# FNet mixing and a gated convolution FFN on one core: weight narrowing spread over two steps, w_in quarters laid end to end, four table loads on another queue

## The chip, the core and the metric

The kernel runs on one core of a Trainium2 chip. The metric is device time in microseconds (us) of one execution. The kernel before was run three times; a further execution was taken by the hardware profiler, and all readings of the trace below are from that one.

## What is computed

Eight sequences of 3136 rows and 256 features (float32) go through a two-dimensional Fourier transform of which the real part is kept, and then through a gated feed-forward layer with a three-tap convolution along the sequence.

```python
X = np.fft.fft(x, axis=1)          # x: (8, 3136, 256)
X = np.fft.fft(X, axis=2)
x = X.real.astype(np.float32)
h = np.maximum(x @ w_in, 0.0)      # w_in: (256, 1024)
hp = pad(h, 1 row on both sides)
conv_out = sum(conv_w[k] * hp[:, k:k + S, :] for k in range(3))
gate = 1.0 / (1.0 + np.exp(-conv_out))
return (h * gate @ w_out)          # w_out: (1024, 256)
```

The activations are float32. The three weight arrays arrive as float64, as pairs of 32-bit words in memory; the kernel turns them into float32 on the chip with integer instructions. This is the "narrowing" below.

## The kernel before, in words

**The work.** For each of the 8 batches the sequence transform is done with matmuls against cosine and sine tables after VectorE has folded the input by symmetry (`fold_ops`, L142). The result lies in two tiles `pt` and `qt` (`PQ[b]`). The transform along the features is multiplied into `w_in` beforehand: `blocks(i)` (L735) multiplies quarter i of `w_in` by the feature tables `dm`, and the product is `G`; `column(i)` (L746) makes the small companion `ge`. One row of the transform is handled apart, by class `Feature` (L468) for batches 1 to 7.

**The main loop** (L1025) runs over steps, one for each batch b, chunk c of the sequence (4 chunks, three of 768 rows and a last one of 832) and block f of 128 hidden features (8 blocks): 256 steps. It is software pipelined. In cycle t these functions are called in this order:

- `sigmoid(t-4)` (L824) on ScalarE
- `products(t+1)` (L777) on TensorE: the two pairs of matmuls into `pb` and `pa`; then `copies(t+1)` (L784) on ScalarE, from `pb` to `nb`
- the side work filed under "first" and "act"
- `combine(t)` (L792) on VectorE, two instructions, giving `h`; `seed(t+2)` (L764) on ScalarE, which starts `pa` of a later step; `first_tap(t)` (L801) on ScalarE, into `g`
- the side work filed under "dve"
- `last_tap(t-3)` (L810) on VectorE; `gate(t-4)` (L830), half on GpSimd (L836), half on VectorE (L837)
- `row_of(t+1)` and `middle(t)` (L806): GpSimd issues a DMA that adds `h` to `g` in SBUF (the middle tap)
- the side work filed under "pool" and "load"
- `mm2(t-5)` (L846): 12 to 14 output matmuls into `po`, and after every eighth step the copies and stores of the results
- the side work filed under "pe"

Each engine takes its instructions strictly in this order of the program, and so does each DMA queue (SP is SyncE's queue, ACTq ScalarE's). The order is written by hand: `at(cycle, where, fn)` (L936) files side work, and `taken` holds the cycles in which VectorE gets no folding of a later batch.

**Around the start of the loop.** `w_in` is narrowed in four quarters (`w4[0..3]`, in two tiles `win` of two quarters each), `w_out` in four pieces of two blocks. `narrow` (L606) has two parts when it is given spare room for the sign: `power` (an integer instruction on VectorE, L620, then a Relu on ScalarE, L622) and `product` (L634 and L635, then L628, which needs the Relu, then L638, all on VectorE). Quarter 1 is narrowed just ahead of the loop, quarter 2 in cycle 0, quarter 3 in cycle 2, and the pieces of `w_out` in cycles 4, 6, 8 and 10: `power` as "first" and `product` as "dve" of the same cycle (L942 to L948). `blocks(1)`, `blocks(2)` and `blocks(3)` come as "pe" in cycles 0, 1 and 3 (L939).

The two quarters of one `win` tile are interleaved: a quarter is two runs of 256 columns, 512 columns apart, one for each half of the contraction:

```python
win = [pqp.tile([P, NK], F32, name="win", tag=tag)[:, 0:F].rearrange("p (t n) -> p t n", t=2)
w4 = [win[i // 2][:, :, i % 2 * N4:(i % 2 + 1) * N4] for i in range(4)]
```

`Feature.place` (L474) is called in cycle 5 under "load". It makes two columns of signs (GpSimd iota L494, VectorE L496, GpSimd L497), clears four short rows on GpSimd (L505) and starts four table loads from ScalarE's queue (L507). `Feature.gather` (L511, on SP) follows in cycles 6 to 8 for batches 1 to 3, element by element; the tables are used from cycle 11 on, the gathered columns in cycle 14.

Of the kernel before, what the change touches and what calls it, by code (L numbers as in the profile page):

```python
# [9 lines left out]
F32 = mybir.dt.float32  # L10
I32 = mybir.dt.int32
U32 = mybir.dt.uint32
AF = mybir.ActivationFunctionType
ALU = mybir.AluOpType
# [16 lines left out]
NQ = 8  # L31
# [6 lines left out]
def kernel(  # L38
# [10 lines left out]
    nc = tc.nc  # L49
    B, S, D = x.shape  # L50
    F = moe_w_in.shape[1]
    P = 128
# [5 lines left out]
    NK = M + 1  # L58
# [17 lines left out]
    pqp = ctx.enter_context(tc.tile_pool(name="pqp", bufs=2))  # L76
# [391 lines left out]
    class Feature:  # L468
# [5 lines left out]
        def place(self):  # L474
            H, t = self.H, erp.tile([P, NK], F32, name="ft", tag="er")
            at_ = [0]

            def take(*sh):
                n = 1
                for v in sh:  # L480
                    n *= v
                v = t[:, at_[0]:at_[0] + n]
                at_[0] += n
                return v
            self.ta = take(2, H + 1).rearrange("p (s k) -> p s k", s=2)
            self.tm = take(2, 2, H).rearrange("p (s r i) -> p s r i", s=2, r=2)
            self.tw = [take(2, 2, H).rearrange("p (s r i) -> p s r i", s=2, r=2) for _ in range(2)]
            self.y = take(4, RC).rearrange("p (b n) -> p b n", b=4)
            self.z = [take(4, 2, RC).rearrange("p (b n) -> p b n", b=4) for _ in range(2)]

            self.sign = take(2)
            odd = self.sign.bitcast(I32)
            for i in range(2):
                nc.gpsimd.iota(odd[:, i:i + 1], pattern=[[0, 1]], base=i, channel_multiplier=1,  # L494
                               allow_small_or_imprecise_dtypes=True)
            nc.vector.tensor_scalar(out=odd, in0=odd, scalar1=1, scalar2=None, op0=ALU.bitwise_and)  # L496
            nc.gpsimd.tensor_scalar(out=self.sign, in0=odd, scalar1=-2.0, scalar2=1.0, op0=ALU.mult, op1=ALU.add)  # L497

            f = t[:, at_[0] - 16 * RC - 2:at_[0] - 2]
            n = (RC + NQ - 1) // NQ  # L500
            self.l = [f[:, 0:2 * HE].rearrange("p (s i) -> p s i", s=2),
                      f[:, 2 * HE:2 * HE + 2 * H].rearrange("p (s i) -> p s i", s=2)]
            for r, v in enumerate(self.l):
                for s in range(2):
                    nc.gpsimd.memset(v[0:1, s], 1.0 - s)  # L505
                    w = v.shape[2]
                    nc.scalar.dma_start(out=v[1:1 + n * NQ, s], in_=bass.AP(  # L507
                        tensor=dft_seq.tensor, offset=dft_seq.offset + (2 * r + s) * NQ * HE,
                        ap=[[4 * NQ * HE, n], [HE, NQ], [1, w]]))

        def gather(self, b, b0):  # L511
            nc.sync.dma_start(out=self.y[self.K, b - b0].unsqueeze(2), in_=bass.AP(
# [93 lines left out]
    def narrow(dst, raw, room=None):  # L606


        ts = nc.vector.tensor_scalar
        lsl, lsr = ALU.logical_shift_left, ALU.logical_shift_right  # L610
        lo, hi = raw[:, :, :, 0], raw[:, :, :, 1]
        lof, d = lo.bitcast(F32), dst.bitcast(I32)
        sg = hi
        if room is not None:
            c, n = hi.shape[1:]
            sg = room[:, 0:c * n].rearrange("p (c n) -> p c n", c=c)

        def power():

            ts(out=d, in0=hi, scalar1=20, scalar2=0x7FF, op0=lsr, op1=ALU.bitwise_and)  # L620
            if room is not None:
                act(d, d, AF.Relu, scale=2.0 ** 23, bias=low[0:d.shape[0]])  # L622
            else:
                ts(out=d, in0=d, scalar1=-896, scalar2=0, op0=ALU.add, op1=ALU.max)
                ts(out=d, in0=d, scalar1=23, scalar2=None, op0=lsl)

        def sign():
            stt(out=d, in0=hi, scalar=-0x80000000, in1=d, op0=ALU.bitwise_and, op1=ALU.bitwise_or)  # L628

        def product():  # L630

            if room is None:
                sign()
            ts(out=sg, in0=hi, scalar1=0xFFFFF, scalar2=0x100000, op0=ALU.bitwise_and, op1=ALU.bitwise_or)  # L634
            stt(out=lof, in0=lo.bitcast(U32), scalar=2.0 ** -32, in1=sg, op0=ALU.mult, op1=ALU.add)  # L635
            if room is not None:
                sign()
            stt(out=dst, in0=lof, scalar=2.0 ** -20, in1=dst, op0=ALU.mult, op1=ALU.mult)  # L638
        return power, product

    class Weight:

# [18 lines left out]
        def narrow(self, c0, c1):  # L661
# [10 lines left out]
                   allow_small_or_imprecise_dtypes=True)  # L672
    nc.gpsimd.tensor_scalar(out=half, in0=half, scalar1=0.5, scalar2=0.5, op0=ALU.mult, op1=ALU.add)
    H = F // 2
    win = [pqp.tile([P, NK], F32, name="win", tag=tag)[:, 0:F].rearrange("p (t n) -> p t n", t=2)
           for tag in ("pt", "qt")]
    w_cv = Weight(cw24, moe_conv_w.rearrange("k (m p) -> (k m) p", m=NF).unsqueeze(1),
                  lambda sh: gp.tile(sh, I32, name="raw", tag="g"))

    dm = gp.tile([P, 2, 2, P], F32, name="dm", tag="g")  # L680
    N4 = F // 4
    w4 = [win[i // 2][:, :, i % 2 * N4:(i % 2 + 1) * N4] for i in range(4)]
    raws = [None, None]

    def raw_in(i):
        def f(sh):
# [5 lines left out]
    w_in = [Weight(w4[i], moe_w_in[:, i * N4:(i + 1) * N4].rearrange("(t p) n -> p t n", p=P), raw_in(i))  # L692
            for i in range(4)]
# [41 lines left out]
    def blocks(i):  # L735

        w = w4[i]
        for g in range(2):
            p = spare()
            for t in range(2):  # L740
                mm(p[:, 0:N4], dm[:, t, g, :], w[:, t], t == 0, t == 1)
            nc.scalar.copy(out=G[:, g, i * N4:(i + 1) * N4], in_=p[:, 0:N4])
        if i > 1:
            column(i)

    def column(i):  # L746

        w, p = w4[i], spare()
        for m in range(NF // 4):
            for t in range(2):  # L750
                mm(p[:, m:m + 1], w[:, t, m * P:(m + 1) * P], dm[:, t, 1, P - 1:P], t == 0, t == 1)
        nc.scalar.copy(out=ge[:, i * NF // 4:(i + 1) * NF // 4], in_=p[:, 0:NF // 4])
# [31 lines left out]
    def copies(s):  # L784

        ch, n, fs = cut(s)
        p = pb.pop(s)
        nb[s] = nbp.tile([P, 2, HN], F32, name="nb", tag="nb")
        for i, cols in enumerate((ch.fcols, ch.cols)):
            act(nb[s][:, i, cols], p[:, cols], AF.Copy, scale=-1.0 if i else 1.0)  # L790
# [107 lines left out]
    for i in range(4):  # L898
        for j, u in enumerate(odds):
            u.part(i)  # L900
            if i == 3:
                u.copy()
                u.fin()
                if j == 1:
                    row()
                    w_out = Weight(wout, moe_w_out.rearrange("(c p) o -> p c o", p=P),
                                   lambda sh: xp.tile(sh, I32, name="raw", tag="xh"))
# [11 lines left out]
    n = chunks[0].k1  # L919
    p = psd.tile([P, 512], F32, name="pd", tag="pd")  # L920
# [7 lines left out]
    room = left[:, NF // 2:].rearrange("p f i -> p (f i)").bitcast(I32)  # L928
# [5 lines left out]
    taken = set()  # L934

    def at(cycle, where, fn):  # L936
        side.setdefault((cycle, where), []).append(fn)

    for i in (1, 2, 3):  # L939
        at((0, 0, 1, 3)[i], "pe", lambda i=i: blocks(i))  # L940

    def shared(cycle, w, c):  # L942
        for where, fn in zip(("first", "dve"), w.parts(c, c + 2, room)):
            at(cycle, where, fn)

    for cycle, w_, c in ((0, w_in[2], 0), (2, w_in[3], 0), (4, w_out, 0), (6, w_out, 2), (8, w_out, 4), (10, w_out, 6)):
        shared(cycle, w_, c)
        taken.add(cycle)  # L948
    for j, fn in enumerate(load_ops(1, 1, nc.sync)):
        at(NF + 3 + max(j - 2, 0), "load", fn)  # L950

# [9 lines left out]

    feat = Feature()
    at(5, "load", feat.place)
    for c, b0, b1 in ((6, 1, min(4, B)), (21, 4, B)):
        for b in range(b0, b1):
            at(c + b - b0, "load", lambda b=b, b0=b0: feat.gather(b, b0))
# [7 lines left out]
    for b in range(1, B):  # L974
# [4 lines left out]
        n = per * b - (2 if b == 1 else 3) - c0  # L979
# [12 lines left out]
    for b in range(1, B):  # L992
        ops, singles, pres = fold_ops(b)
        c0, n = ends[b - 1], ends[b] - ends[b - 1]
# [4 lines left out]
        else:  # L999
            if b == 2:  # L1000
                c0, n = c0 + 3, n - 3
# [16 lines left out]
    n = len(steps)  # L1018
# [2 lines left out]
    seed(steps[1])  # L1021
    products(steps[0])
    copies(steps[0])
    column(1)
    for t in range(n + LAG):  # L1025
        def run(where):
            for fn in side.get((t, where), []):
                fn()
        if 0 <= t - 4 < n:
            sigmoid(steps[t - 4])  # L1030
        if t + 1 < n:
            products(steps[t + 1])
            copies(steps[t + 1])
        run("first")
        run("act")
        if t >= LAG:
            keep(steps[t - LAG])
        if t < n:
            combine(steps[t])
        if t + 2 < n:  # L1040
            seed(steps[t + 2])
        if t < n:
            first_tap(steps[t])

        run("dve")
        if 0 <= t - 3 < n:
            last_tap(steps[t - 3])
        if 0 <= t - 4 < n:
            gate(steps[t - 4])
        if t + 1 < n:  # L1050
            row_of(steps[t + 1])
        if t < n:
            middle(steps[t])
        run("pool")
        run("load")
        if t >= LAG:
            mm2(steps[t - LAG])
        run("pe")
# [66 lines left out]
```

## Time and profile before

| | |
|---|---|
| median of 3 runs | 1173.87 us (1173.63, 1173.87, 1175.4) |
| the profiled execution | 1175.2 us |
| its span in the trace | 1173.4 us |
| TensorE busy with matmuls | 1139.6 us, 97% of the span |
| VectorE, ScalarE, GpSimd busy | 83%, 80%, 52% |
| TensorE clock granted, mean over the span | 0.998 |
| DMA traffic | 168.15 MB, 143 GB/s in the mean |

In the lines quoted below, PE is TensorE's matmuls, DVE VectorE, ACT ScalarE, POOL GpSimd. A line of the timeline has the start in us, the duration in us, the engine, the line of the kernel, the operation with its tiles and shapes, the number of instructions merged into the line, and in brackets the idle time ahead of it with what ended it. All matmuls are issued from L93; their tiles tell them apart: `po<-wout,g` are the output matmuls of `mm2`, `pb<-qt,G` and `pa<-pt,G` those of `products`, `po<-win,dm` those of `blocks`. A line of the waits has the total in us, the number of waits and the longest of them.

### The profile page before, as it was taken

How to read it: one execution, taken by the hardware profiler on the slowest of the kernel's cores; microseconds unless marked ns; L12 is line 12 of the kernel's file. 1: busy time of each engine (PE TensorE's matmuls, PEld its weight loads, DVE VectorE, ACT ScalarE, POOL GpSimd, SP SyncE). 2: the span in 40 equal slices, each digit the busy share in tenths (PEclk: the TensorE clock that was granted, in tenths of full speed). 3: DMA queues.
4: the chain of work that ended last, by engine and by line, in shares of the span. 5: the costliest groups of instructions: out<-in, count | busy, mean ns of one | idle time of the engine just before them, and what ended most of it. 6: DMA issues, size and time to landing. Idle time of an engine off the chain costs nothing.

```text
span 1173.4 us, 15901 instructions
## 1 busy us (share of the span) xinstructions
PE 1139.6 (97%) x4818; PEld 887.5 (76%) x4818; DVE 970.7 (83%) x1448; ACT 942.9 (80%) x1939; POOL 606.9 (52%) x734
## 2 busy tenths in 40 slices
PE   4889999999999999999999999999999999999998
PEld 2756777778778777777777777777778777777777
DVE  7589979998788789798886888889787778788885
ACT  2578868888788888888887878888887888898885
POOL 5346755666465554756455464654344344444443
PEclk9999999999999999999999999999999999999999
DMA  8777787776677676667676676865665656666654
GB/s 209 192 108 156 165 138 165 160 162 135 141 159 168 136 169 141 147 135 176 144 166 139 122 149 141 177 126 121 135 120 107 126 122 142 130 130 129 126 116 102
DMA packets 106050, 168.15 MB, mean 143 GB/s; under 512 B 31121, under 2 KB 61091, under 8 KB 105965
## 3 DMA queue, kind: packets, MB, share of 16 engines
q0 software_dynamic: 41984, 115.83, 51.7%
q1 hardware_dynamic: 62809, 50.88, 15.8%
q8 instruction: 38, 0.62, 0.2%
q10 hardware_dynamic: 1172, 0.43, 0.2%
q14 instruction: 47, 0.39, 0.1%
HBM read 38.40 MB, written 25.74 MB: 55 GB/s over the span
## 4 chain that ended last, share of the span: by engine, by line
PE 77%; ACT 4%; DVE 3%; issue 1%; DMA 0%; POOL 0%; ACTq 0%; DVEq 0%
PE po L93 49%; PE pb L93 12%; PE pa L93 11%; PE pd L93 6%; ACT nb L790 1%; DVE g L813 1%; ACT os L861 1%; ACT g L828 1%; DMA out_dram<-os 0%; ACT pa L769 0%; DVE g L837 0%; DVE w L228 0%; DVE xh L168 0%; ACT g L804 0%; DVE pt L418 0%
## 5 line engine op out<-in xcount | busy, mean ns | idle before, releaser
L93 PE MATMUL po<-wout,g 128*128 128x256 f32 x3072 | 708.3, 380 | 6.6 <-DVE g L837 5.8
L93 PEld LDWEIGHTS po<-wout,g 128*128 128x128 f32 x3072 | 581.6, 190 | 152.5 <-issue 19.7
L808 POOL DMA_DIRECT2D g<-h x256 | 227.7, 889 | 464.5 <-ACT g L804 270.6
L828 ACT ACTIVATE g<-g,cw 128x385 f32<-128x385 f32 (+2 forms) x512 | 292.3, 625 | 68.1 <-DVE g L813 65.5
L836 POOL TENSOR_TENSOR g<-g,h 128x385 f32<-128x385 f32 (+1 forms) x256 | 301.2, 1177 | 49.5 <-ACT g L828 47.9
L790 ACT ACTIVATE nb<-pb 128x386 f32<-128x386 f32 (+3 forms) x512 | 227.3, 499 | 112.1 <-PE pb L93 111.4
L798 DVE CUSTOM_DVE_ANT_0 h<-pa,nb 128x386 f32<-128x386 f32 (+3 forms) x512 | 264.3, 556 | 29.3 <-POOL h L775 19.8
L813 DVE SCALAR_TENSOR_TENSOR g<-h,cw,g 128x770 f32<-128x770 f32 (+1 forms) x256 | 282.8, 1105 | 0.0
L804 ACT ACTIVATE g<-h,cw 128x770 f32<-128x770 f32 (+1 forms) x256 | 244.4, 955 | 0.0
L93 PE MATMUL pb<-qt,G 127*128 127x387 f32 (+2 forms) x512 | 214.0, 499 | 2.6 <-ACT nb L790 1.1
L93 PE MATMUL pa<-pt,G 128*128 128x387 f32 (+2 forms) x512 | 212.3, 495 | 1.2 <-ACT pa L769 1.2
L837 DVE TENSOR_TENSOR g<-g,h 128x385 f32<-128x385 f32 (+1 forms) x256 | 187.0, 730 | 25.0 <-ACT g L828 24.8
L769 ACT ACTIVATE pa<-eb,ge 128x387 f32<-128x387 f32 (+2 forms) x256 | 155.4, 607 | 1.3 <-DVE h L798 1.0
L93 PEld LDWEIGHTS pa<-pt,G 128*128 128x128 f32 x512 | 96.4, 189 | 76.4 <-issue 17.4
L132 POOL DMA_INDIRECT xh<-in_x_dram,idx x64 | 91.1, 1423 | 18.5 <-issue 12.2
L93 PE MATMUL pd<-tab,w 98*128 98x197 f32 (+2 forms) x448 | 98.0, 318 | 0.8 <-DVE w L228 0.7
L93 PEld LDWEIGHTS pb<-qt,G 127*128 127x128 f32 x512 | 90.8, 190 | 9.7 <-ACT nb L790 2.7
L93 PEld LDWEIGHTS pd<-tab,w 98*128 98x128 f32 (+1 forms) x448 | 81.8, 191 | 10.5 <-DVE w L228 1.0
L861 ACT COPY os<-po 128x256 f32<-128x256 f32 x196 | 57.4, 395 | 6.5 <-PE po L93 6.5
L168 DVE TENSOR_TENSOR xh<-xh 98x1024 f32<-98x1024 f32 (+1 forms) x32 | 47.4, 1482 | 0.1
L157 DVE TENSOR_TENSOR xh<-xh 98x1020 f32<-98x1020 f32 (+1 forms) x32 | 46.9, 1471 | 0.0
L385 DVE TENSOR_TENSOR as<-as,pd 128x196 f32<-128x196 f32 x14 | 5.0, 358 | 38.0 <-ACT as L381 38.0
(140 smaller groups left out, 447.7 us busy)
## 6 DMA issues: line engine op xcount, KB each, us to landing
g<-h POOLq DMA_DIRECT2D x192, 385.0 KB, 4.1
g<-h POOLq DMA_DIRECT2D x64, 416.0 KB, 4.4
out_dram<-os SPq DMA_DIRECT2D x96, 256.0 KB
xh<-in_x_dram SPq DMA_DIRECT2D x16, 784.0 KB
eb<-ed SPq DMA_DIRECT2D x16, 193.5 KB
raw<-in_moe_w_in_dram SPq DMA_DIRECT2D x4, 512.0 KB
raw<-in_moe_w_out_dram SPq DMA_DIRECT2D x1, 2048.0 KB
eb<-ed SPq DMA_DIRECT2D x8, 209.0 KB
```

The lines of the kernel that those rows point to most:

```text
L93: nc.tensor.matmul(o, l, r, start=start, stop=stop, skip_group_check=True)
L132: nc.gpsimd.indirect_dma_start(out=xh[b, h][0:NP, 7 - m].rearrange("p q d -> p (q d)"), out_offset=None, in_=bass.AP(tensor=x.tensor, offs ...
L769: act(pa[s][:, 0:n], eb[b, c], AF.Copy, scale=ge[:, f:f + 1])
L790: act(nb[s][:, i, cols], p[:, cols], AF.Copy, scale=-1.0 if i else 1.0)
L798: nc.vector._custom_dve(TENSOR_ADD_SAT, out=to, in0=a[:, cols], in1=c[:, i, cols], s0=BIG, s1=0.0)
L804: act(gs[s], hs[s][:, 0:n], AF.Copy, scale=cw[:, 0, s[2]:s[2] + 1])
L808: nc.gpsimd.dma_start(out=gs[s], in_=hs[s][:, 1:1 + n], accum_op=ALU.add)
L813: stt(out=g, in0=h[:, k:k + n], scalar=cw[:, k, f:f + 1], in1=g, op0=ALU.mult, op1=ALU.add)
L828: act(gs[s][:, c], gs[s][:, c], AF.Sigmoid, scale=cw[:, 1, s[2]:s[2] + 1])
L836: gt(g[:, p], g[:, p], h[:, p], op=ALU.mult)
L837: vt(g[:, v], g[:, v], h[:, v], op=ALU.mult)
L861: nc.scalar.copy(out=osb[:, j % 2], in_=pt[:, j % 2])
```

## The change

It has four parts.

1. The quarters of `w_in` lie one behind the other in their tiles, so that each quarter is one run of 512 columns.
2. `narrow` with room gives three parts in place of two: the last two VectorE instructions (L628 and L638) become `value`, and `value` is filed one cycle after `power` and `product`. For quarter 3 and for `w_out`, `power` and `product` move one cycle earlier (to cycles 1, 3, 5, 7, 9), and `value` takes the cycle where all of it stood (2, 4, 6, 8, 10). For quarter 2, `power` moves ahead of the loop; `product` and `value` stay in cycle 0.
3. `blocks(1)` moves from the end of cycle 0 to ahead of the loop, behind `column(1)`, and so ahead of `products` of step 1.
4. In `Feature`, the four table loads are started from SP's queue; the two sign instructions L496 and L497 are called in cycle 8 under "dve" and no longer in `place`.

```diff
-            nc.vector.tensor_scalar(out=odd, in0=odd, scalar1=1, scalar2=None, op0=ALU.bitwise_and)
-            nc.gpsimd.tensor_scalar(out=self.sign, in0=odd, scalar1=-2.0, scalar2=1.0, op0=ALU.mult, op1=ALU.add)
...
-                    nc.scalar.dma_start(out=v[1:1 + n * NQ, s], in_=bass.AP(
+                    nc.sync.dma_start(out=v[1:1 + n * NQ, s], in_=bass.AP(
...
+        def signs(self):
+            odd = self.sign.bitcast(I32)
+            nc.vector.tensor_scalar(out=odd, in0=odd, scalar1=1, scalar2=None, op0=ALU.bitwise_and)
+            nc.gpsimd.tensor_scalar(out=self.sign, in0=odd, scalar1=-2.0, scalar2=1.0, op0=ALU.mult, op1=ALU.add)
...
             stt(out=lof, in0=lo.bitcast(U32), scalar=2.0 ** -32, in1=sg, op0=ALU.mult, op1=ALU.add)
+            if room is None:
+                value()
+
+        def value():
             if room is not None:
                 sign()
             stt(out=dst, in0=lof, scalar=2.0 ** -20, in1=dst, op0=ALU.mult, op1=ALU.mult)
-        return power, product
+        return (power, product) if room is None else (power, product, value)
...
-    win = [pqp.tile([P, NK], F32, name="win", tag=tag)[:, 0:F].rearrange("p (t n) -> p t n", t=2)
+    win = [pqp.tile([P, NK], F32, name="win", tag=tag)[:, 0:F].rearrange("p (i t n) -> p i t n", i=2, t=2)
...
-    w4 = [win[i // 2][:, :, i % 2 * N4:(i % 2 + 1) * N4] for i in range(4)]
+    w4 = [win[i // 2][:, i % 2] for i in range(4)]
...
-    for i in (1, 2, 3):
+    for i in (2, 3):
         at((0, 0, 1, 3)[i], "pe", lambda i=i: blocks(i))
-    def shared(cycle, w, c):
-        for where, fn in zip(("first", "dve"), w.parts(c, c + 2, room)):
-            at(cycle, where, fn)
-    for cycle, w_, c in ((0, w_in[2], 0), (2, w_in[3], 0), (4, w_out, 0), (6, w_out, 2), (8, w_out, 4), (10, w_out, 6)):
-        shared(cycle, w_, c)
-        taken.add(cycle)
+    early, *rest = w_in[2].parts(0, 2, room)
+    for fn in rest:
+        at(0, "dve", fn)
+    for cycle, w_, c in ((1, w_in[3], 0), (3, w_out, 0), (5, w_out, 2), (7, w_out, 4), (9, w_out, 6)):
+        for j, where, fn in zip((0, 0, 1), ("first", "dve", "dve"), w_.parts(c, c + 2, room)):
+            at(cycle + j, where, fn)
+    taken.update((0, 2, 4, 6, 8, 10))
...
     at(5, "load", feat.place)
+    at(8, "dve", feat.signs)
...
     copies(steps[0])
+    early()
     column(1)
+    blocks(1)
```

## The prediction

> **What bounds the kernel now.** First the shares on the page, to see which engine could set the end.
>
> ```profile
> PE 1139.6 (97%) x4818; PEld 887.5 (76%) x4818; DVE 970.7 (83%) x1448; ACT 942.9 (80%) x1939; POOL 606.9 (52%) x734
> ```
>
> TensorE is the bound nearly everywhere, so a gain must come from the few stretches in which it waits, and the change touches only the ramp and the first eleven steps (about 45 to 100 us). Next, the chain near the end shows what a step costs when TensorE is fed, and TensorE's timeline shows how the early steps differ.
>
> ```profile
> 1103.63 2.59 PE po L93 x12
> 1106.22 0.65 PE pb L93 x2
> 1106.88 0.65 PE pa L93 x2
> ```
>
> ```profile
> 70.23 2.86 PE L93 MATMUL po<-wout,g 128*128 128x256 f32 x12 [1.46 <-DVE g L837]
> ...
> 80.41 4.49 PE L93 MATMUL po<-wout,g 128*128 128x256 f32 x12 [1.97 <-DVE g L837]
> ...
> 98.67 2.86 PE L93 MATMUL po<-wout,g 128*128 128x256 f32 x12 [0.63 <-DVE g L837]
> ...
> 112.08 2.75 PE L93 MATMUL po<-wout,g 128*128 128x256 f32 x12
> ```
>
> A fed step takes 2.59 + 0.65 + 0.65 = 3.89 us. The first output matmuls (step 0) start at 70.23, those of step 6 at 98.67: 28.44 us for six steps where 23.3 would do, so 5.1 us are lost. From 98.67 to 112.08, three steps later, 1.7 us more go. Each of the three waits shown names VectorE's half of the gate: in these steps the bound is VectorE. Its waits between 45 and 100 us say why.
>
> ```profile
> DVE win L620 <- PE po L93: 4.9, 2, 3.6
> DVE wout L628 <- ACT wout L622: 2.1, 2, 1.2
> DVE ft L496 <- POOL ft L494: 1.8, 1, 1.8
> DVE win L628 <- ACT win L622: 1.1, 1, 1.1
> ```
>
> That is 9.9 us of standing still on the engine everything waits for. The first row is a write to one quarter of w_in waiting for matmuls that read the other quarter: the quarters interleave, and the order between them is kept as if they overlapped. Rows two and four are the narrowing waiting for its own Relu. Row three is the sign column waiting for GpSimd.
>
> **Part 1, the waits that go.** Laid end to end, the quarters share no range and the first row goes. Of its 4.9 us, 3.6 are the wait of quarter 3, which stops VectorE in cycle 2. The other 1.2, ahead of the loop, gain almost nothing: the Relu stands on ScalarE behind copies that end when it now starts. With value one cycle later, the Relu has a whole cycle, so rows two and four (3.2 us) go. Signs in cycle 8 find their iota done (1.8 us). What does VectorE need without waits?
>
> ```profile
> 80.28 1.02 DVE L798 CUSTOM_DVE_ANT_0 h<-pa,nb 128x385 f32<-128x385 f32 x2
> ...
> 82.70 0.41 DVE L620 TENSOR_SCALAR wout<-raw 128x512 int32<-128x512 int32 x1
> ...
> 93.46 0.41 DVE L620 TENSOR_SCALAR wout<-raw 128x512 int32<-128x512 int32 x1
> ...
> 98.53 1.02 DVE L798 CUSTOM_DVE_ANT_0 h<-pa,nb 128x386 f32<-128x386 f32 x2
> ```
>
> A plain step runs from 80.28 to 82.70, 2.42 us; a step with a whole narrowing and no wait from 93.46 to 98.53, 5.07. Two steps take 7.49, or 3.75 each, and the split spreads this evenly. That is just below TensorE's 3.89. So once the waits are gone, TensorE takes over as the bound. What is late next is ScalarE, in the ramp.
>
> **Part 2, the ramp.** Here the change adds something: blocks(1) now stands ahead of the products of step 1.
>
> ```profile
> 51.06 1.89 PE L93 MATMUL po<-win,dm 128*128 128x256 f32 x8
> 51.37 0.72 ACT L622 ACTIVATE win<-win,low 128x512 int32<-128x512 int32 x1
> 51.98 0.59 ACT L769 ACTIVATE pa<-eb,ge 128x386 f32<-128x386 f32 x1
> 52.13 0.69 DVE L628 SCALAR_TENSOR_TENSOR win<-raw,win 128x512 int32<-128x512 int32 x1 [1.15 <-ACT win L622]
> 52.49 0.94 ACT L804 ACTIVATE g<-h,cw 128x770 f32<-128x770 f32 x1
> 52.85 0.69 DVE L638 SCALAR_TENSOR_TENSOR win<-raw,win 128x512 f32<-128x512 f32 x1
> 53.32 0.64 ACT L742 COPY G<-po 128x256 f32<-128x256 f32 x2
> ```
>
> The 1.89 us push the products of step 1, their copies, the seed and the first tap back; 0.3 us from the earlier narrowing and the 0.7 of the Relu, which leaves its place ahead of the seed, come off. The first tap of step 0 then starts near 53.3 in place of 52.49: 0.8 us lost, the price of this edit. From there I laid the engines out by hand with the spacing of ScalarE's instructions in a stretch where it never waits:
>
> ```profile
> 116.70 1.11 ACT L828 ACTIVATE g<-g,cw 128x385 f32<-128x385 f32 x2
> 117.72 0.85 ACT L790 ACTIVATE nb<-pb 128x386 f32<-128x386 f32 x2
> 118.46 0.57 ACT L769 ACTIVATE pa<-eb,ge 128x387 f32<-128x387 f32 x1
> 118.97 0.93 ACT L804 ACTIVATE g<-h,cw 128x770 f32<-128x770 f32 x1
> 119.80 1.11 ACT L828 ACTIVATE g<-g,cw 128x385 f32<-128x385 f32 x2
> ```
>
> Start to start: sigmoid 1.02, copies 0.74, seed 0.51, first tap 0.83. From the first tap of step 0 to the end of the first tap of step 4, which is followed by sigmoid(1), ScalarE has 5 taps (4.15), 4 pairs of copies (2.96), 4 seeds (2.04), 2 Relus (0.6 each to the next start, 1.2), 2 sets of copies of G with ge (1.6) and one sigmoid (1.02): 13.0 us. Hence sigmoid(1) near 66.3, the seed of step 6 done near 65.6, its products near 66.5, and the output matmuls of step 0 right behind, at **66.5 in place of 70.23: 3.7 us** gained. VectorE's half of gate(0) lands near 66.3 by the same layout, so neither is far ahead. Bounds: 70.23 + 0.8 if ScalarE alone had set the old ramp, 65.6 if nothing of the ramp waited for TensorE. I take 66.5 because ScalarE is laid out back to back.
>
> **Part 3, steps 0 to 6.** From there TensorE should run at 3.89 a step. Of the 5.1 us lost before I keep 1.0: one refill, and one wait in step 10, because in step 9 a fold instruction of batch 1 falls in with power, product and an ordinary step on VectorE. Step 6 then starts near 66.5 + 23.3 + 1.0 = 90.8, **4.1 us** gained. The ends are 0 (all lost again to something else) and 5.1. The stretched 4.49 us at 80.41 belong to it: the granted clock was halved there.
>
> ```profile
> 76.00:80.00 4.00, 2.45 (x9) 1.21 (x7) 3.93 (x6) 2.41 (x6) 1.81 (x3) 1.00 0.20 35
> 80.00:84.00 4.00, 3.59 (x9) 2.91 (x10) 4.00 (x9) 4.00 (x8) 1.43 (x2) 0.57 0.53 99
> ```
>
> The columns are PE, PEld, DVE, ACT, POOL busy, then the granted clock, which is 0.57 in the second stretch after one in which TensorE was busy 2.45 of 4 us. The 12 matmuls took 4.49 in place of 2.86, 1.63 more. Without the wait of 1.97 ahead of it the first stretch is full and this goes too. The Trainium skill, "TensorE: Matmul & The Clock Gate" (Part 1), has the clock drop only after about a whole 3.4 us window of idleness; by that rule this drop should not have come at all, and the trace goes against it. By the rule the changed kernel runs at full clock throughout, as in my sum; by the trace it could be halved wherever TensorE is half idle, which is a rival below.
>
> **Part 4, what I cost at nothing.** Four table loads move to SP's queue, ahead of the gathers.
>
> ```profile
> L507 ACTq DMA_DIRECT2D ft<-dft_seq_dram x4: 761/782/862, 71.2 to 73.7; - x4
> ```
>
> ```profile
> L512 SPq DMA_DIRECT2D ft<-in_x_dram x3: 902/5281/7396, 49.2 to 57.6; - x3
> ```
>
> Four issues of 0.78 us leave ScalarE, 3.1 us. They add nothing to my sum because ScalarE is not the bound by then; if it is, they are a gain of up to 3.1. On SP they go out near 49 us, when SP is already free, and push the three gathers back by 3.1 us; these are read only in cycle 14, and behind them SP has nothing until the load of cycle 11. Without that cover the price is 3.1 us once. L497 now makes GpSimd wait for VectorE in cycle 8, and its half of gate(4) and the tap's DMA queue behind it; VectorE has last_tap and its own half to do meanwhile, which hides it. The layout changes no duration: every quarter keeps 512 columns an instruction. Value one cycle later still ends a cycle ahead of the output matmuls that use it.
>
> **The sum.** 3.7 + 4.1 = 7.8 us, against the profiled execution's own 1175.2: **1167.4**. Later steps are bound by TensorE, so the gain stays. The profiled execution lies 1.3 us above the median of 1173.87; the halved clock may be that difference, or not. If it is, 1167.4 holds as it stands; if the profile simply costs 1.3, it is 1166.1. Best case: the ramp gains 3.7, all 5.1 come back, and the 1.7 of steps 6 to 9 too, 10.5 us, or 1164.7.
>
> **The rivals.**
>
> A: the clock is halved once more, in the thinner ramp. Price 1.63, time 1169.0. For it: the row above. Against: the layout has TensorE busier than before in each stretch from 52 us on.
>
> B: the middle tap's DMA becomes the late one.
>
> ```profile
> DMA to landing us min/median/max: 7.3/7.3/7.3
> ```
>
> That is the tap of step 0, issued while the gathers run. The gathers now end 3.1 us later, so the next two taps also meet them, and VectorE asks for each tap earlier. In the layout the tap of step 1 lands within half a microsecond of its use. If landings grow by the 3.1, the ramp gives 3 us back: 1170.4.
>
> C: the change doesn't do what it says: quarters stay tied to each other by tile and not by range. Then blocks(2) waits for the Relu of quarter 3, about 1.2 us later on TensorE, and ScalarE's chain inherits it: 1168.6.
>
> D: VectorE stays the bound, because its integer instructions meet GpSimd.
>
> ```profile
> L634 DVE TENSOR_SCALAR left<-raw x7: 409/419/1524, 46.2 to 94.7; 128x512 int32<-128x512 int32 x7
> ```
>
> The same instruction takes 0.42 in the median and up to 1.52. The slack of 3.89 - 3.75 is 0.14 a step, so three such meetings (1.1 each) more than now cost 3 us: 1170.4. The Trainium skill, "Advanced Engine Details and Errata" (VectorE Performance Modes, Mode Summary), says that VectorE's second port is shared with GpSimd and that two-port instructions block each other; it speaks against filing these instructions in other cycles, and the spread of this row agrees with it.
>
> E, slower: the halved clock feeds itself. Matmuls of the ramp at half speed delay copies, seeds and gates, TensorE idles, and the next stretch is halved too. Each costs about 1.63, so from the fifth on (7.8 / 1.63) the gain is eaten; at seven the time is 1178.8 with no gain elsewhere than forecast. For it: one such stretch exists. Against: it did not repeat even after the 1.97 wait.
>
> **How the numbers follow.** Forecast 0.61 (1164.5 to 1169), A 0.08, B 0.12, C 0.07, D 0.09, E 0.03. A measurement of this kernel tells about 0.2% from no change, 2.3 us. Faster by more: the forecast, A, C, and most of B and D, 0.92. Within: the dear ends of B and D, 0.05. Slower: E, 0.03. The range 1163.8 to 1170.8 takes in the best case with half a microsecond, and B and D at their price.
>
> **What would show it.** VectorE's waits L620 for TensorE, L628 for the Relu and L496 for the iota are gone; output matmuls start near 66.5 and those of step 6 near 90.8; the granted clock stays 1.00 from 20 us on; L507 stands on SP near 49 to 53. I am wrong if the first start is later than 68, if waits of last_tap for its DMA appear, or if VectorE shows no idle time in steps 2 to 9 while TensorE waits for L837.

## The result and the profile after

The changed kernel takes 1170.03 us in the median of 8 runs (1168.57 to 1171.95), the kernel before 1174.61 in 8 runs beside it (1173.62 to 1176.98). The ratio is 0.9959, with a 95% interval from 0.9947 to 0.9971: 4.6 to 4.8 us faster. The profiled execution took 1169.77 us against 1175.2, 5.4 less. The forecast was 1167.4, a gain of 7.8. The sign and the range held; the sum was 2.4 us too large against the profiled execution, and 3.0 to 3.2 against the medians. The median lies above the band of 1164.5 to 1169 that the forecast itself was given, close to the 1170.4 of rivals B and D.

VectorE's waits between 45 and 100 us in the changed kernel, to be held against the four rows of before (line numbers are higher by 4 to 9: L620 is now L624, L628 is L632, L634 is L638, `last_tap` is L822, the gate's halves are L845 and L846):

```profile
DVE g L822 <- DMA g<-h: 1.7, 1, 1.7
DVE win L632 <- ACT win L626: 0.9, 1, 0.9
DVE h L807 <- POOL h L784: 0.8, 1, 0.8
DVE h L807 <- PE pa L93: 0.7, 2, 0.5
```

9.9 us have become 4.1. The four rows of before are gone from the loop: the waits for the matmuls of the other quarter, for the iota, and the two rows for the Relu. Ahead of the loop 0.9 us stand in place of 1.2, now for a Relu that stands behind other copies. The other rows are new: the last tap of step 0 waits 1.7 us for the accumulating DMA, and `combine` (L807) of the first steps waits 1.5 us, for GpSimd's clear of the edges of `h` and for matmuls. Next, TensorE's output matmuls of steps 0, 2, 5, 6 and 9:

```profile
67.59 2.86 PE L93 MATMUL po<-wout,g 128*128 128x256 f32 x12 [0.81 <-DVE g L846]
...
76.40 2.86 PE L93 MATMUL po<-wout,g 128*128 128x256 f32 x12 [0.76 <-DVE g L846]
...
89.86 2.86 PE L93 MATMUL po<-wout,g 128*128 128x256 f32 x12 [1.50 <-DVE g L846]
93.86 2.75 PE L93 MATMUL po<-wout,g 128*128 128x256 f32 x12
...
107.14 2.75 PE L93 MATMUL po<-wout,g 128*128 128x256 f32 x12
```

The first group starts 2.6 us earlier than before (70.23), that of step 6 4.8 us earlier (98.67), that of step 9 4.9 us earlier (112.08). The gain is made before 94 us and then kept. The last output matmuls on the chain that ends last, before and after:

```profile
1147.75 20.73 PE po L93 x96
```

```profile
1142.33 20.73 PE po L93 x96
```

They start 5.4 us earlier. TensorE, busy 97% of the span before and after, passes what is gained in the ramp on to the end, as was forecast.

Between step 0 and step 6 26.27 us pass, where 28.44 passed before, 24.3 were forecast and 23.3 would be the work alone. All three bracketed waits are for VectorE's half of the gate: VectorE is still the bound of these steps, though from 62.2 us on it no longer stands still in them. What holds it is seen when GpSimd's instructions are shown beside its own. The changed kernel, VectorE and GpSimd, as step 6 begins:

```profile
71.78 0.54 POOL L494 IOTA ft<- 128x1 int32 x2
...
71.94 0.90 POOL L503 MEMSET ft<- 1x393 f32 x4
72.12 2.10 DVE L632 SCALAR_TENSOR_TENSOR wout<-raw,wout 128x512 int32<-128x512 int32 x1
...
72.81 0.86 POOL L845 TENSOR_TENSOR g<-g,h 128x385 f32<-128x385 f32 x1
```

L632, the first instruction of `value`, was L628 in the kernel before and needed 0.69 us there for every piece of `w_out` (the times are in ns):

```profile
L628 DVE SCALAR_TENSOR_TENSOR wout<-raw,wout x4: 684/692/696, 67.4 to 95.8; 128x512 int32<-128x512 int32 x4
```

Here it takes 2.10 and ends 0.5 us after GpSimd has finished its clears and its gate. The same again in steps 8 and 9, first GpSimd, then VectorE:

```profile
82.51 0.88 POOL L513 TENSOR_SCALAR ft<-ft 128x2 f32<-128x2 int32 x1 [1.61 <-DVE ft L512]
83.37 1.17 POOL L845 TENSOR_TENSOR g<-g,h 128x385 f32<-128x385 f32 x1
84.48 0.87 POOL L817 DMA_DIRECT2D g<-h  x1
85.09 1.16 POOL L845 TENSOR_TENSOR g<-g,h 128x385 f32<-128x385 f32 x1
```

```profile
83.73 1.09 DVE L624 TENSOR_SCALAR wout<-raw 128x512 int32<-128x512 int32 x1
84.74 1.01 DVE L807 CUSTOM_DVE_ANT_0 h<-pa,nb 128x386 f32<-128x386 f32 x2
85.68 0.86 DVE L638 TENSOR_SCALAR left<-raw 128x512 int32<-128x512 int32 x1
```

The sign instruction makes GpSimd wait 1.61 us for VectorE; its gate of step 4 comes late, the gate of step 5 right behind it, and both lie over integer instructions that take 0.42 us when nothing is beside them. L807 between them, which reads PSUM and one SBUF tile, is not stretched (1.01 us). The size of it all can be added up from VectorE's timeline: from its half of gate(0) at 66.98 to that of gate(5) at 89.25 VectorE works without a gap, 22.3 us for five steps. 2.5 of these are stretch (1.41 in L632, 0.67 in L624, 0.44 in L638); without them a step would take VectorE 3.95 us, beside TensorE's 3.89.

### The profile page after: what moved, and what is told of

Same layout as the page of the kernel before. It is cut to its first block, busy times and chain, and to the rows that moved or that the text cites. A ratio compares the mean times of both kernels' runs of the same rounds, so it can differ in the third digit from the quotient of the medians.

```text
span 1168.0 us, 15901 instructions
## 1 busy us (share of the span) xinstructions
PE 1136.9 (97%) x4818; PEld 886.9 (76%) x4818; DVE 970.5 (83%) x1448; ACT 942.1 (81%) x1939; POOL 610.3 (52%) x734
## 4 chain that ended last, share of the span: by engine, by line
PE 78%; ACT 4%; DVE 3%; issue 2%; DMA 0%; POOL 0%; ACTq 0%; DVEq 0%
PE po L93 49%; PE pb L93 12%; PE pa L93 12%; PE pd L93 6%; ACT nb L799 1%; ACT os L870 1%; DVE g L822 1%; ACT g L837 1%; ACT pa L778 0%; ACT g L813 0%; DMA out_dram<-os 0%; DVE g L846 0%; DVE h L807 0%; DVE w L228 0%; DVE pt L418 0%
## 5 line engine op out<-in xcount | busy, mean ns | idle before, releaser
L845 POOL TENSOR_TENSOR g<-g,h 128x385 f32<-128x385 f32 (+1 forms) x256 | 303.7, 1187 | 49.9 <-ACT g L837 48.2
L807 DVE CUSTOM_DVE_ANT_0 h<-pa,nb 128x386 f32<-128x386 f32 (+3 forms) x512 | 264.6, 557 | 31.2 <-POOL h L784 20.6
L822 DVE SCALAR_TENSOR_TENSOR g<-h,cw,g 128x770 f32<-128x770 f32 (+1 forms) x256 | 282.8, 1105 | 1.7 <-DMA g<-h 1.7
L846 DVE TENSOR_TENSOR g<-g,h 128x385 f32<-128x385 f32 (+1 forms) x256 | 187.2, 731 | 24.8 <-ACT g L837 24.7
```

The costliest lines, as they stand in the source:

```text
L807: nc.vector._custom_dve(TENSOR_ADD_SAT, out=to, in0=a[:, cols], in1=c[:, i, cols], s0=BIG, s1=0.0)
L822: stt(out=g, in0=h[:, k:k + n], scalar=cw[:, k, f:f + 1], in1=g, op0=ALU.mult, op1=ALU.add)
L845: gt(g[:, p], g[:, p], h[:, p], op=ALU.mult)
L846: vt(g[:, v], g[:, v], h[:, v], op=ALU.mult)
```

## The experiments

The theory after the result: the split of the narrowing carries the gain; 1.2 us were lost because the gathers, pushed back by the table loads, make the first tap's DMA late; 2 us because GpSimd's work now lies over VectorE's two-input and integer instructions. The rivals: the layout carried the gain; or what looks like lost time is only step 9, which is long by itself.

The runs of one kernel spread by 2 to 4 us, and the next two fences show a reason. They are the stretch from 32 to 36 us, ahead of everything the change touches, in the changed kernel and in the kernel with the loads back on ScalarE's queue (columns: PE, PEld, DVE, ACT, POOL busy, granted clock, DMA share, GB/s).

```profile
32.00:36.00 4.00, 4.00 (x25) 4.00 (x24) 0.86 (x3) 0.84 (x3) 0.00 (x0) 1.00 0.54 193
```

```profile
32.00:36.00 4.00, 4.00 (x17) 4.00 (x17) 0.00 (x0) 0.00 (x0) 0.00 (x0) 0.67 0.11 41
```

The clock is halved for part of this stretch in the second execution (0.67 in the mean of the 4 us) and not in the first, though both have the same program up to there; the matmuls of the first `column` (`po<-dm,win`) start at 42.77 in the first and at 44.32 in the second, 1.55 us later. Of the 14 profiled executions, 8 had such a stretch in the first 100 us, one of them two. So the times of a few runs do not separate kernels that differ by 1 us, and the readings below rest also on the traces: the start of the output matmuls of step 0 and of step 6, counted from the matmuls of the first `column`. "Ratio" is to the kernel before. The last column is the fastest execution on record of each kernel, in us; its mean granted clock is 0.999 or 1.000 in every kernel, where one stretch takes 0.0015 off (half of 3.4 us in 1168). The kernel before was run beside each group of the others; its fastest there are 1173.42 to 1173.83. The two fastest of a kernel lie within 0.3 us of each other in all but u_signs and signs_dve.

```text
kernel         ratio, 95% interval       step 0   step 6   halved clock, first 100 us   fastest
before         1                         27.32    55.76    at 80                        1173.42
the change     0.9959 [0.9947, 0.9971]   24.82    51.09    none                         1168.57
u_layout       0.9965 [0.9952, 0.9978]   25.00    51.52    at 31, ahead                 1170.08
u_split        0.9990 [0.9981, 0.9999]   26.88    54.57    at 70                        1172.73
u_queue        0.9943 [0.9931, 0.9955]   23.59    49.69    at 31, ahead                 1168.10
u_signs        0.9958 [0.9945, 0.9971]   25.27    51.97    at 44                        1168.95
u_blocks       0.9960 [0.9947, 0.9973]   23.74    50.27    none                         1169.00
q_behind       0.9956 [0.9943, 0.9969]   23.59    50.11    none                         1168.64
place_early    0.9956 [0.9943, 0.9969]   23.59    49.46    none                         1168.08
signs_dve      0.9962 [0.9950, 0.9974]   24.55    50.65    none                         1168.54
cheap_gather   0.9961 [0.9947, 0.9975]   23.59    50.10    none                         1169.05
split_only     0.9974 [0.9964, 0.9984]   26.61    53.30    at 44                        1170.55
best           0.9953 [0.9939, 0.9967]   25.27    50.68    at 43                        1168.25
best_blocks    0.9949 [0.9935, 0.9962]   25.44    50.85    at 32 and 45                 1167.99
```

"Ahead" means ahead of the counted part.

**Which part carries the gain.** First each part undone, the others kept.

```diff
# u_split
-    early, *rest = w_in[2].parts(0, 2, room)
-    for fn in rest:
-        at(0, "dve", fn)
-    for cycle, w_, c in ((1, w_in[3], 0), (3, w_out, 0), (5, w_out, 2), (7, w_out, 4), (9, w_out, 6)):
-        for j, where, fn in zip((0, 0, 1), ("first", "dve", "dve"), w_.parts(c, c + 2, room)):
-            at(cycle + j, where, fn)
+    for cycle, w_, c in ((0, w_in[2], 0), (2, w_in[3], 0), (4, w_out, 0), (6, w_out, 2), (8, w_out, 4), (10, w_out, 6)):
+        for where, fn in zip(("first", "dve", "dve"), w_.parts(c, c + 2, room)):
+            at(cycle, where, fn)
...
-    early()
```

> The change with the narrowing filed as before (power, product and value in one cycle, quarter 2's power in cycle 0), the other parts kept. Theory: VectorE waits for its own Relu again, about 3 us in all, and narrowing steps are long; 2 to 3 us slower than the change, ratio near 0.998. Rival (the split only moved VectorE's work under GpSimd's, and the stretched 2.10 and 1.30 us instructions ate what it gained): within 1 us of the change, ratio 0.996.

The ratio is 0.9990: of the 0.41% that the change gains, 0.31% go, 3.6 us; between the fastest executions it is 4.2. Its trace has the waits that the split takes away:

```profile
DVE win L632 <- ACT win L626: 5.3, 3, 2.9
DVE wout L632 <- ACT wout L626: 2.2, 3, 1.2
```

Step 6 starts 3.5 us later than in the change, with a halved stretch on the way (4.54 for twelve output matmuls in place of 2.86, 1.7 us). The rival, that the split only moved work under GpSimd's, is out.

```diff
# u_layout
-    win = [... .rearrange("p (i t n) -> p i t n", i=2, t=2)
+    win = [... .rearrange("p (t n) -> p t n", t=2)
-    w4 = [win[i // 2][:, i % 2] for i in range(4)]
+    w4 = [win[i // 2][:, :, i % 2 * N4:(i % 2 + 1) * N4] for i in range(4)]
```

> The change with its first part undone: the quarters of w_in interleave again. Theory (the split and the earlier filing already take quarter 3 off the matmuls of the ramp): now blocks(2) waits for the Relu of quarter 3 and value of quarter 3 for column(2), about 1 us on the ramp; 1.0 us slower than the change, ratio to the kernel before near 0.997. Rival (the layout was the main gain, its 3.6 us wait comes back whole): 3 us or more slower than the change, ratio 0.999.

0.9965, 0.7 us slower in the ratio and 0.4 us in the trace at step 6: the theory's side, though the ratios alone do not separate it from the change. The trace makes the layout look too cheap: last_tap of step 0 does not wait for its DMA here, as it does for 1.7 us in the change. Against q_behind below, where that wait is gone too, this kernel is 1.4 us late both at step 0 and at step 6, and its two fastest executions (1170.08 and 1170.10) are 1.5 us slower than the fastest of the change. The waits are back, the 1.2 us ahead of the loop whole, that of quarter 3 short, because it is now filed a step earlier:

```profile
DVE win L632 <- PE po L93: 1.4, 1, 1.4
DVE win L624 <- PE po L93: 1.2, 1, 1.2
```

Of the wait of 3.6 us that the prediction put down to the interleaving, earlier filing alone thus removes most; 1.4 are left, now ahead of `value`. The split alone, with everything else as before:

```diff
# split_only: the kernel before, and of the change only part 2
```

> The kernel before with the second part of the change alone (narrowing over two steps, one step earlier, quarter 2's power ahead of the loop); quarters interleaved, blocks(1) at the end of step 0, loads on ScalarE, signs in the placing. Theory (this part carries nearly the whole gain, and the others give and take within 1.5 us): 4 to 5 us faster than the kernel before, ratio 0.996, like the whole change. Rival (the parts need each other: with interleaved quarters VectorE or TensorE waits in the ramp and the split gains half): ratio 0.998.

0.9974: 3.1 us of the 4.8, between the two expectations; between the fastest executions 3.3 (1173.83 beside it to 1170.55). Its profiled execution has a halved stretch in the ramp, so its step 0 and step 6 are late by some 1.7 us. The split stands without the other parts, and with the 1.4 to 1.5 us of the layout it makes up nearly the whole gain.

**The table loads on SP.**

```diff
# u_queue
-                    nc.sync.dma_start(out=v[1:1 + n * NQ, s], in_=bass.AP(
+                    nc.scalar.dma_start(out=v[1:1 + n * NQ, s], in_=bass.AP(
```

> The change with the four table loads back on ScalarE's queue. Theory (prediction): nothing is lost, since the sigmoid of step 2 waits for VectorE longer than the issues take; within 0.5 us of the change, ratio 0.996. Rival 1: ScalarE is held 1.6 us in step 5 or 6 and the gate of step 2 comes later; 1 to 1.5 us slower, ratio 0.997. Rival 2: the gathers start 3.6 us earlier on SP, the first tap lands earlier, and the kernel is up to 1 us faster than the change.

0.9943, the fastest ratio of all, though its interval meets that of the change; between the fastest executions it is 0.5 us. In the trace step 6 starts 1.4 us earlier than in the change. The wait of last_tap for its DMA is not there. This is rival 2, and in these traces it speaks against a part of the change. SP's queue in the changed kernel, and VectorE at the tap:

```profile
48.41 3.56 SPq L505 DMA_DIRECT2D ft<-dft_seq_dram  x4
52.01 16.91 SPq L516 DMA_DIRECT2D ft<-in_x_dram  x3
```

```profile
62.23 1.02 DVE L822 SCALAR_TENSOR_TENSOR g<-h,cw,g 128x770 f32<-128x770 f32 x1 [1.73 <-DMA g<-h]
```

The gathers run from 52.0 to 68.9 in place of 49.2 to 62.8. The tap's DMA was issued at 54.3 and VectorE goes on at 62.2, 7.9 us later, where the DMA of the kernel before had landed after 7.3. To test the reason, the loads were put behind the gathers:

```diff
# q_behind: the loads of place as a method of their own
+    at(9, "load", feat.loads)
```

> The change with the four table loads on SP behind the three gathers (filed in step 9) instead of ahead of them. Theory (ahead of the gathers they push these 3.6 us later, the accumulating DMA of the first tap lands late under them, and VectorE stands 1.7 us at last_tap of step 0): that wait is gone and the output matmuls of step 0 start about 1.2 us earlier; 1.2 to 1.6 us faster than the change, ratio to the kernel before 0.9945. Rival (the gain with the loads on ScalarE's queue was the chance of that chip): same as the change, 0.996.

```profile
48.31 13.28 SPq L521 DMA_DIRECT2D ft<-in_x_dram  x3
61.63 6.71 SPq L510 DMA_DIRECT2D ft<-dft_seq_dram  x4
```

The wait is gone, step 0 starts 1.2 us earlier and step 6 1.0 earlier in two executions at full clock. The times (0.9956 against 0.9959) do not show it, and the fastest execution of the change, 1168.57, is as fast as that of q_behind, 1168.64. So the change probably does not wait for this DMA in every execution; that is not shown, since no trace here is of one that doesn't. And with the gathers made cheap in pieces (the kernel then reads 56 neighbouring features of every 56th row, and leaves out the one feature of every row that is needed):

```diff
# cheap_gather
-    ap=[[RC * D, RC], [D, RC], [1, 1]]
+    ap=[[RC * D, RC], [1, RC]]
```

> The change with the gathers reading 56 neighbouring elements a row in place of 56 elements a row's length apart: the same bytes in far fewer pieces; it leaves out that the right feature is gathered. Theory (the element-wise gathers make the accumulating DMAs of the first taps land late): the first tap lands within 5 us in place of 7.9, the wait of 1.7 us at last_tap of step 0 is gone, output matmuls of step 0 start near 66.3; 1 us faster than the change, ratio 0.995. Rival (the late landing is the fill of the DMA engines by other loads): the landing stays above 7 us and so does the wait.

The three gathers now take SP 2.9 us in place of 16.9, the wait is gone, and step 0 starts 1.2 us earlier, as with the loads behind them. The ratio, 0.9961, does not show it, against 0.995 expected. The landing itself is not shown in the traces of these three kernels, only the wait. Its length differs between executions: 1.7 us in the change, 1.4 in signs_dve and 0.5 in place_early, with the same order on SP, and each of these kernels has one trace. So the traces side with the theory that the element-wise gathers behind the loads make that DMA late, but how they do it stays open: in q_behind element-wise gathers run beside the same DMA, from 48.3 to 61.6, and VectorE does not wait.

**blocks(1) ahead of the loop.**

```diff
# u_blocks
-    for i in (2, 3):
+    for i in (1, 2, 3):
...
-    blocks(1)
```

> The change with blocks(1) back at the end of step 0, behind the products of step 1. Theory (blocks(1) ahead costs ScalarE's chain 0.6 us at the first tap, and the ramp hangs on ScalarE and the first tap's DMA): 0.5 us faster than the change in the ramp. Rival (behind the products its copies of G hold up the products of step 2, as the 1.1 us wait of TensorE on G in the kernel before): 0.5 to 1 us slower.

Step 0 starts 1.1 us earlier than in the change, step 6 0.8 earlier; the ratio is the same, and the fastest execution is 0.4 us slower. The trace goes in the theory's direction, by more than its 0.5: GpSimd issues the first tap at 52.50 and not at 54.34, so that it lands in time.

```profile
52.50 1.01 POOL L817 DMA_DIRECT2D g<-h  x1 [5.53 <-ACT G L751]
```

In the traces, the loads behind the gathers or back on ScalarE's queue, cheap gathers, and blocks(1) undone thus all take away one and the same wait, 1.1 to 1.2 us at step 0; they do not add up.

**GpSimd beside VectorE.**

```diff
# place_early
-    at(5, "load", feat.place)
...
     blocks(1)
+    feat.place()
```

> The change with the placing (iota, the four clears, the loads) called ahead of the loop, where GpSimd is idle, so that GpSimd has nothing in step 5 but its gate and tap; the signs stay in step 8, SP's order stays. Theory (GpSimd's work of step 5 lies over VectorE's L632 of step 6, which took 2.10 us in place of 0.69): L632 is short again, the wait of 0.8 us ahead of the third output matmuls goes; 0.5 to 0.8 us faster than the change, ratio 0.9955. Rival (TensorE's wait at step 10 absorbs whatever comes earlier): no difference, 0.996, with that wait longer by what was gained.

VectorE in step 6 of this kernel, then TensorE at steps 1, 2 and 5:

```profile
71.58 0.97 DVE L632 SCALAR_TENSOR_TENSOR wout<-raw,wout 128x512 int32<-128x512 int32 x1
```

```profile
70.79 2.86 PE L93 MATMUL po<-wout,g 128*128 128x256 f32 x12 [0.28 <-DVE g L846]
74.79 2.81 PE L93 MATMUL po<-wout,g 128*128 128x256 f32 x12
...
88.22 2.86 PE L93 MATMUL po<-wout,g 128*128 128x256 f32 x12 [1.52 <-DVE g L846]
```

With GpSimd's clears out of step 5, L632 falls from 2.10 to 0.97 and the wait ahead of the third group goes. Step 6 starts 1.6 us earlier: 1.2 at step 0, by the shorter wait for the tap, and 0.4 after it. The wait of step 5's output matmuls does not grow, so the rival (step 10 absorbs the gain) falls. The ratio does not show the gain; the fastest execution is 0.5 us faster. Not all of the stretch is gone: beside GpSimd's earlier gates the last tap of step 1 takes 1.62 us here in place of 1.00, and L638 of step 5 1.12.

```diff
# signs_dve
-            nc.gpsimd.tensor_scalar(out=self.sign, in0=odd, scalar1=-2.0, scalar2=1.0, ...)
+            nc.vector.tensor_scalar(out=self.sign, in0=odd, scalar1=-2.0, scalar2=1.0, ...)
```

> The change with the second sign instruction on VectorE, so that GpSimd waits for nothing in step 8. Theory (GpSimd's gate of step 4, held behind its sign instruction until 83.4, and the next one meet L624 and L638 of step 9 and stretch them by 1.1 us in all): these two are 0.42 us each again, the wait of 1.50 us ahead of the output matmuls of step 5 falls below 0.7; 0.7 to 1.0 us faster than the change, ratio 0.995. Rival (step 9 is long by its fold instruction alone): that wait stays at 1.5 and the time at 0.996.

```profile
80.72 1.42 DVE L632 SCALAR_TENSOR_TENSOR wout<-raw,wout 128x512 int32<-128x512 int32 x1
...
84.45 0.42 DVE L624 TENSOR_SCALAR wout<-raw 128x512 int32<-128x512 int32 x1
84.79 1.02 DVE L807 CUSTOM_DVE_ANT_0 h<-pa,nb 128x386 f32<-128x386 f32 x2
85.73 0.41 DVE L638 TENSOR_SCALAR left<-raw 128x512 int32<-128x512 int32 x1
```

L624 and L638 are short again and the wait ahead of step 5's output matmuls falls from 1.50 to 0.70, as expected. But GpSimd's gate, no longer held back, now meets L632 of step 8, 1.42 in place of 0.68. The gain is 0.4 us at step 6, of which 0.3 stand already at step 0 (a shorter wait for the tap), and not the 0.7 to 1.0 expected; the time shows nothing. A meeting avoided in one step is met in the next. The 0.70 us ahead of step 5 stay in u_signs, best and best_blocks as well, so this part of step 9 is long by itself, as the rival has it.

```diff
# u_signs
+            self.signs()
...
-    at(8, "dve", feat.signs)
```

> The change with the two sign instructions back in the placing of step 5. Theory (in step 8 the GpSimd one holds up the gates behind it, and they then stretch L624 to 1.09 and L638 to 0.86 us): what VectorE loses in step 5 (1.8 us of waiting) it mostly regains in step 9; within 0.7 us of the change. Rival (prediction's reckoning: 1.8 us of wait come back and nothing else changes): 1.5 to 1.8 us slower, ratio 0.9975.

0.9958, the ratio of the change. The theory's side: the move of the signs by itself brings nothing that the ratio shows. Its trace shows VectorE waiting 0.7 us for the iota, where the kernel before waited 1.8.

**Put together.**

```diff
# best: place ahead of the loop, loads behind the gathers, both sign instructions on VectorE
-    at(5, "load", feat.place)
-    at(8, "dve", feat.signs)
+    at(2, "dve", feat.signs)
+    at(9, "load", feat.loads)
...
     blocks(1)
+    feat.place()
```

> The change with GpSimd's placing work ahead of the loop, the table loads on SP behind the gathers, and both sign instructions on VectorE in step 2. Theory: no wait on the first tap's DMA, no long L632 in step 6; the signs cost nothing in step 2; with GpSimd free in step 8 L632 of step 8 is stretched instead of L624 and L638 of step 9; output matmuls of step 0 near 66.3, of step 6 near 92; 1.5 to 2 us faster than the change, ratio 0.9943. Rival (TensorE's wait at step 10 eats it): ratio 0.9955.

> The kernel called best here, with blocks(1) back at the end of step 0. Theory (blocks(1) ahead costs about 1 us in the ramp only where the first tap's DMA is late, since the chain then runs through that tap): with the loads behind the gathers it makes less than 0.5 us, ratio 0.994 as the kernel without this edit. Rival (it costs ScalarE's chain its 0.6 us in any case): 0.6 to 1 us faster, ratio 0.9937.

0.9953 and 0.9949, medians 1169.27 and 1170.13 us, fastest runs 1168.25 and 1167.99 (the change: 1168.57). Both profiled executions had a halved stretch in or ahead of the ramp. From step 0 to step 6 they need 25.4 us, against 26.27 in the change. In the trace of best the wait for the tap's DMA is gone, L632 takes 0.97 in step 6 and 1.43 in step 8, and L624 and L638 of step 9 take 0.42 and 0.41, as expected (all three stand 5 lines lower in this kernel); but L638 of step 5 takes 1.67 in their place. As times, neither is shown to beat the change, and they are not shown to differ from each other.

## Why the prediction was right, and where its sum was off

**What bounds the kernel** held: VectorE's waits in the first eleven steps, and TensorE carrying the gain to the end (4.8 us at step 6, 5.4 at the end). Two of the three signs that the prediction named for being wrong came all the same: last_tap waits for its DMA, and from step 4 on VectorE has no idle time while TensorE waits for its half of the gate. That the time still fell into the range is owed to the width of the range, which takes in rivals B and D.

**Part 1, the waits that go**, held for all four rows. The attribution was too simple: the 3.6 us wait of quarter 3 was put down to the layout; u_layout shows that filing it a step earlier removes most of it. The conclusion that TensorE takes over as the bound once the waits are gone did not hold (Part 3).

**Part 2, the ramp**, said 66.5 and 3.7 us; 67.59 and 2.6 us came. The first tap came at 53.1 where 53.3 was laid out. The step that failed is that no wait for its DMA stands in the layout: VectorE asked for it 6.2 us after the issue (at 60.5) and went on after 7.9, with sigmoid, copies and gate behind it. Already with the 7.3 us of before it would have waited 1.1. Without that wait (q_behind, cheap_gather) step 0 starts near 66.3 to 66.7, where the layout by hand had it. Rival B was thus right in kind, for one tap and with 1.2 us in place of 3.

**Part 3, steps 0 to 6**, is the largest error: "of the 5.1 us lost before I keep 1.0" was 2.9. The work of VectorE was summed with each instruction's undisturbed duration, so that 3.75 us a step came out, below TensorE's 3.89; with 2.5 us of stretch in five steps it was 4.45. Rival D had the right mechanism and named one kind of instruction too few: not only the integer TENSOR_SCALARs, also the two-input L632 is stretched, from 0.69 to 2.10, where the kernel before never showed it. place_early and signs_dve show the mechanism by moving GpSimd's work; as a size it rests on the sum, since the best arrangement tried got back only 0.9 of the 1.9 us. The halved clock at 80 us did not come back in the change's profile; since it comes and goes between executions of the same program, that it went because of the change is not shown. The 4.1 us of Part 3 contain its 1.63. Without it the forecast gain is 6.2, and the fastest executions of the two kernels, whose mean clock of 1.000 leaves no room for such a stretch, are 4.9 apart (1173.42 and 1168.57).

**Part 4, what was costed at nothing**, failed for the table loads. The cover named was for whoever reads the gathers, and that held; what the gathers run beside was left to rival B. The price was about 1.2 us in the profiled execution; in the fastest, which are no slower than those of q_behind, it was probably less. The sign instruction on GpSimd was costed at nothing because VectorE's work hides its wait; TensorE did not see the wait, but it delayed two gates into VectorE's way (signs_dve). The 1.8 us of Part 1 for the iota brought no gain in time (u_signs).

**Rivals A and E**: the halved stretch is a draw of each execution, not of the kernel; u_signs and best have one in the ramp and start step 0 1.7 us later than q_behind does. Each cost about the 1.63 that was laid out. best_blocks alone has two, with about 10 us at full clock between them; whether the first brought on the second is not shown, and none of the 14 has more.

## What to carry to other kernels

Count for a moved transfer not only who waits for it but what else is in flight at its new time: here four small loads ahead of element-wise gathers cost 1.2 us in the profiled execution, at a consumer of neither, and no run shows a gain from the queue that they left. When an engine's waits are removed, sum its work with the durations it has beside its neighbours, not with the undisturbed ones; a schedule without waits packs instructions of VectorE and GpSimd over each other. Several causes of one wait do not add: four different edits each removed the same 1.2 us, and the wait hid 1.4 us that the layout was worth. And where executions of one program differ, look at the fastest ones before a wait in a single trace is given a price.

## What was not expected of the hardware

- The granted clock was halved for a stretch of 3.4 us (0.57 in the mean of 4 us at 80 in the kernel before) in 8 of 14 profiled executions, at 31, 43 to 45, 70 or 80 us. One such stretch cost 1.55 us ahead of the loop and 1.7 in the ramp. Identical programs up to that point had it or not. What brings it on stays open: five of the nine stretches came after 3.4 us in which TensorE was busy for 1.4 to 1.8 us, but the four at 43 to 45 after 3.4 us in which the profile has it busy throughout, as here in u_signs, where the first 3.7 us of the second row run at full clock:

```profile
36.00:40.00 4.00, 4.00 (x39) 3.26 (x38) 3.60 (x10) 1.99 (x7) 0.23 (x1) 1.00 0.03 8
40.00:44.00 4.00, 4.00 (x25) 3.21 (x24) 2.76 (x8) 1.77 (x5) 3.51 (x6) 0.96 0.93 303
```

- An instruction of VectorE with two SBUF inputs (L632) took 0.69 us alone and 2.10 with GpSimd's iota, clears and gate beside it.
- Three gathers of 3136 single elements held SP's queue for 11.1 to 17.9 us in the 13 kernels that have them, and 2.9 us when the same bytes lay in 56 runs each.
